# Sixteen dummy matmuls ahead of the first transposes, and a zeroing moved from GpSimd to VectorE

## The chip, the cores and the metric

The kernel runs on one core of one Trainium2 chip. The metric is the device time of one execution in microseconds (us). In the views PE is TensorE (PEld its weight loads), DVE is VectorE, ACT is ScalarE and POOL is GpSimd; L297 is a line of the kernel, x16 a count, `out<-in` what an instruction writes and reads, and `[0.53 <-...]` how long its engine stood idle before it and what ended that.

## The reference, cut to what matters

Attention over landmarks (Nyström) for 8 batches of 8 heads, 576 tokens and 64 dimensions, then a two-layer MLP with a squared ReLU:

```python
q_lm, k_lm = segment means of q and k          # 32 landmarks
A, Bm, C = sm(q, k_lm), sm(q_lm, k_lm), sm(q_lm, k)   # softmaxes
Z = pseudo-inverse of Bm, six Newton steps
x = A @ Z @ C @ v                               # [...] heads joined
h = x @ w_in; r = maximum(h, 0); return (r * r) @ w_out
```

## The kernel before

The program lays out the whole order of each engine by hand. Batch 0 goes through a "head", a list of tokens, before the steady part begins. In the head these tokens matter: `ck` casts k, `tk1` and `tk0` transpose its halves on TensorE, `mk` and `mq` take the segment means of k and q, `cq0` and `cq1` cast q, `w:n` and `w:n:256` issue n dummy matmuls of 512 or 256 columns.

```python
HEAD = ("ck tk1 mk w:1:256 w:1:256 ek1d w:1:256 w:1 tk0 tt w:1 w:1 cq0 cq1 ek0a mq tq0 tq1 lm ...")

def warm(n, width=512):
    z = bds[1].rearrange("p a b c -> p (a b c)")      # a tile zeroed at the start
    for _ in range(n):
        nc.tensor.matmul(idle[:, 0:width], lhsT=z[:, 0:P], rhs=z[:, 0:width], start=True, stop=True)

# token ck
dve(X["k"][:, 0:2], raw[:, 0:2])                      # half of k on VectorE
load_rest(act(X["k"][:, 2:4], raw[:, 2:4]))           # half on ScalarE; later loads wait for it
```

`load_rest` issues, in GpSimd's queue, the weights, v of batch 0, q and k of batch 1 and v of batch 1. Behind the last of these stands the work that the change moves:

```python
with tc.issue_after(behind[0].ins):
    nc.gpsimd.tensor_copy(seg[:, NC4 + 2, :], seg[:, NC4, :])
    for i in range(2):
        ct = const.tile([P, 2, NC4 + 1, P], BF16, name="ct%d" % i)
        nc.gpsimd.memset(ct[:], 0.0)
        cts.append(ct)
```

The two `ct` tiles are used by `ct = cts[b % 2] if b >= DMA_C else None`, and `DMA_C` is 9, so with eight batches nothing reads them. The other line to know is the VectorE copy that brings a later batch's k or q into its natural order (line 283; 282 in the changed kernel):

```python
nc.vector.tensor_copy(X[nm][:], raw)                  # 128 x 2048 bf16, SBUF to SBUF
```

The softmax here doesn't subtract the row's maximum and nothing guards it: scores larger than these inputs give would overflow.

## Time and profile before

| | kernel before |
|---|---|
| runs before the prediction | 265.61, 265.70, 266.66 us |
| profiled run | 266.55 us, of which the span is 264.8 us |
| TensorE (PE) busy | 248.2 us, 94% |
| first transposes start | 8.01 us |
| first landmark scores (line 374) | 14.29 us |
| copy of batch 1's q on VectorE | 2.54 us, from 27.80 us |

The span counts from the first to the last instruction. The lines behind the table, and how to read them, stand in the prediction.

### The profile page before, as it was taken

Reading aid. Unit: us, or ns where it says so; the run is one execution under the profiler, and the core shown is the slowest. Engines: PE = TensorE matmul, PEld = TensorE weight load, DVE = VectorE, ACT = ScalarE, POOL = GpSimd, SP = SyncE. Lnnn points to the kernel's source line nnn. Section 1 sums busy time; section 2 is a strip of 40 time slices with the busy share of each in tenths; the row PEclk is TensorE's granted clock in tenths of the full one; section 3 lists DMA queues with packets and bytes.
Section 4 is the critical chain, followed back from the end, with each engine's and each line's share of the span. In section 5 each row is a group of like instructions: output and inputs, shape, how many; then the busy total and the mean of one; then the engine's idle time right before and its main releaser. Section 6 shows DMA issues by size and latency. Waiting matters only on the chain.

```text
span 264.8 us, 6918 instructions
## 1 busy us (share of the span) xinstructions
PE 248.2 (94%) x2835; PEld 153.7 (58%) x2878; DVE 176.4 (67%) x485; ACT 158.5 (60%) x278; POOL 47.8 (18%) x73
## 2 busy tenths in 40 slices
PE   0799899999999999999999999999999999999994
PEld 0675665467665656566556565666566655555443
DVE  3488986879985779689766589689776884232100
ACT  1364887279666765678457565674777665365210
POOL 7744623302010500700003201320000000000000
PEclk9999999999999999999999999999999999999999
DMA  8999999998159899996829998999911111112122
GB/s 183 161 190 202 209 205 189 214 208 107 32 101 188 98 197 178 184 203 124 121 74 115 172 192 114 128 191 188 159 42 40 42 40 65 56 40 83 40 79 79
DMA packets 69791, 34.65 MB, mean 131 GB/s; under 512 B 37376, under 2 KB 64256, under 8 KB 69760
## 3 DMA queue, kind: packets, MB, share of 16 engines
q0 software_dynamic: 39808, 17.83, 54.2%
q1 hardware_dynamic: 24704, 7.08, 17.3%
q10 hardware_dynamic: 5248, 9.31, 11.3%
q8 instruction: 22, 0.36, 0.6%
q14 instruction: 9, 0.07, 0.1%
HBM read 36.70 MB, written 9.44 MB: 174 GB/s over the span
## 4 chain that ended last, share of the span: by engine, by line
PE 87%; DVE 5%; DMA 2%; issue 2%; ACT 2%; ACTq 0%
PE ops L853 24%; PE h L824 22%; PE n L853 21%; PE n L532 3%; PE g L807 3%; DMA stage<-in_k_dram 2%; PE idle L297 2%; PE n L416 2%; PE n L344 2%; PE n L598 2%; PE n L616 1%; DVE nat L283 1%; DVE gT L829 1%; PE tps L315 1%; PE n L631 1%
## 5 line engine op out<-in xcount | busy, mean ns | idle before, releaser
L828 ACT ACTIVATE r<-h 128x576 bf16<-128x576 f32 x128 | 81.3, 652 | 46.4 <-PE h L824 35.1
L853 PE MATMUL ops<-w_out_bf,gT 128*128 128x512 bf16 (+1 forms) x300 | 76.8, 368 | 0.9 <-issue 0.3
L853 PEld LDWEIGHTS <-gT 128*128 128x128 bf16 x592 | 53.2, 98 | 38.7 <-issue 4.2
L829 DVE TENSOR_TENSOR gT<-r 128x576 bf16<-128x576 bf16 x128 | 54.9, 448 | 26.3 <-ACT r L828 26.1
L824 PE MATMUL h<-AT,G 128*128 128x288 bf16 x448 | 71.0, 286 | 0.2
L853 PE MATMUL n<-w_out_bf,gT 128*128 128x512 bf16 x252 | 69.7, 379 | 1.1 <-issue 0.3
L824 PEld LDWEIGHTS <-G 128*128 128x128 bf16 x512 | 47.7, 97 | 24.3 <-issue 0.8
L705 DVE CAST G<-g 128x1024 bf16<-128x1024 f32 x14 | 17.1, 1224 | 5.4 <-PE g L807 5.4
L864 ACT COPY o_sb<-ops 128x512 f32<-128x512 f32 (+1 forms) x19 | 10.9, 574 | 14.5 <-PE ops L853 14.5
L864 ACT COPY o_sb<-n 128x512 f32<-128x512 f32 x17 | 10.0, 587 | 12.9 <-PE n L853 12.8
L705 ACT CAST G<-g 128x1024 bf16<-128x1024 f32 x14 | 14.2, 1013 | 4.5 <-PE g L807 4.5
L134 POOL DMA_DIRECT2D raw<-in_k_dram x5 | 4.6, 921 | 53.2 <-DVE gT L829 28.1
L532 PEld LDWEIGHTS <-T 128*128 128x128 bf16 x256 | 11.3, 98 | 4.2 <-issue 0.6
L574 DVE TENSOR_REDUCE ra<-EA 128x20 f32<-128x640 f32 (+3 forms) x19 | 13.2, 704 | 0.3 <-ACT EA L562 0.3
L586 DVE TENSOR_TENSOR an<-EA,rra 128x640 bf16<-128x640 f32 (+2 forms) x18 | 13.2, 736 | 0.2
L532 PE MATMUL n<-bd,T 128*128 128x64 bf16 x256 | 12.7, 193 | 0.3 <-issue 0.2
L315 PEld LDWEIGHTS <-nat 128*128 128x128 bf16 x96 | 6.8, 108 | 9.8 <-ACT nat L720 8.0
L537 ACT ACTIVATE EA<-n 128x512 f32<-128x512 f32 x16 | 9.6, 598 | 3.3 <-PE n L532 3.2
L134 POOL DMA_DIRECT2D raw<-in_q_dram x5 | 4.4, 884 | 38.5 <-DVE rc L447 28.1
L537 ACT ACTIVATE EC<-n 128x512 bf16<-128x512 f32 x16 | 9.5, 596 | 3.0 <-PE n L532 1.6
L315 PE MATMUL tps<-ident_bf,nat 128*128 128x128 bf16 x32 | 3.4, 278 | 8.0 <-ACT nat L720 8.0
L824 PE MATMUL h<-AZ,G 128*128 128x288 bf16 x64 | 10.0, 286 | 0.6 <-DVE AZ L797 0.4
(144 smaller groups left out, 294.6 us busy)
## 6 DMA issues: line engine op xcount, KB each, us to landing
out_dram<-o_sb ACTq DMA_DIRECT2D x31, 256.0 KB, 3.1
vm<-in_v_dram POOLq DMA_DIRECT2D x8, 512.0 KB, 10.1
raw<-in_k_dram POOLq DMA_DIRECT2D x5, 512.0 KB, 6.9
raw<-in_q_dram POOLq DMA_DIRECT2D x5, 512.0 KB, 6.1
w_in_bf<-in_moe_w_in_dram POOLq DMA_DIRECT2D x4, 512.0 KB, 12.1
w_out_bf<-in_moe_w_out_dram POOLq DMA_DIRECT2D x4, 512.0 KB, 17.2
out_dram<-o_sb ACTq DMA_DIRECT2D x9, 128.0 KB, 2.4
stage<-in_k_dram SPq DMA_DIRECT2D x1, 1024.0 KB, 6.1
```

What stands on the lines that cost most here:

```text
L134: d = queue.dma_start(dst, src)
L315: nc.tensor.transpose(tps[:, i, p, :], X[nm][:, 2 * half + i, 2 * p:2 * p + 2, :].rearrange("p h d -> p (h d)"), ident_bf[:],)
L532: nc.tensor.matmul(sc[:, c, j, :, :], lhsT=X[nm + "T"][:, c, p, :], rhs=BD[:, 1 if nm == "q" else 0, p, 0:64], start=True, stop=True)
L537: nc.scalar.activation(dst, sc.rearrange("p c j i m -> p c (j i m)"), AF.Exp, scale=SCALE)
L574: nc.vector.reduce_sum(ra[:, quads, lo:hi, :], EA[:, quads, lo:hi, :].rearrange("p q c (h m) -> p q c h m", m=M), axis=AX.X)
L586: on.tensor_tensor(an[:, i, lo:hi, :].rearrange("p c (h m) -> p c h m", m=M), EA[:, i, lo:hi, :].rearrange("p c (h m) -> p c h m", m=M), r ...
L705: (act, dve)[n % 2](G[:, :, n * 512:n * 512 + 512], gg[:])
L824: nc.tensor.matmul(h[:, j, 0:HALF], lhsT=G[:, qd, f * P:(f + 1) * P], rhs=AT[:, qd, a0 + j * HALF:a0 + (j + 1) * HALF], start=(qd == 0), s ...
L828: nc.scalar.activation(r.rearrange("p (j t) -> p j t", j=2), h[:, :, 0:HALF], AF.Relu)
L829: return lambda: nc.vector.tensor_tensor(gT[:, f, o:o + S], r[:], r[:], ALU.mult)
L853: nc.tensor.matmul(ops, lhsT=gT[:, f, t * P:t * P + P], rhs=w_out_bf[:, f, i * n:i * n + n], start=(f == 0), stop=(f == NF - 1))
L864: nc.scalar.copy(o_h, ops)
```

## The change

Two parts. The dummies are to bring TensorE's clock up while k is still loading, so that k's transposes already run at the rate of the later ones (0.056 us each in the kernel before, where the first took 0.107). The zeroing goes to VectorE, which also only waits for k at that time (idle for 3.42 us ahead of its cast of k in the kernel before).

```diff
 HEAD = (
-    "ck tk1 mk w:1:256 ...
+    "w:16 ck tk1 mk w:1:256 ...
@@ constants, ahead of the first cast
     nc.vector.memset(EA[:, :, NC4, :], 1.0)
+    for i in range(2):
+        ct = const.tile([P, 2, NC4 + 1, P], BF16, name="ct%d" % i)
+        nc.vector.memset(ct[:], 0.0)
+        cts.append(ct)
+    nc.vector.tensor_copy(seg[:, NC4 + 2, :], seg[:, NC4, :])
@@ end of load_rest
-        with tc.issue_after(behind[0].ins):
-            nc.gpsimd.tensor_copy(seg[:, NC4 + 2, :], seg[:, NC4, :])
-            for i in range(2):
-                ct = const.tile([P, 2, NC4 + 1, P], BF16, name="ct%d" % i)
-                nc.gpsimd.memset(ct[:], 0.0)
-                cts.append(ct)
```

## The prediction

The early columns give 2.2 us and the copy 1.86, together 4.1; q's load and PE leave 2.9 of these (264.8 to 261.9 us of span), and half of the 0.9 us that lucky runs may have already is taken off, which makes the gain 2.5 and the time 263.2 us. The 5.7 us in it run from PE's first transposes (8.01 us) to the change of their spacing.

> **What bounds the kernel now.** I read the page's busy shares and chain first, then the chain of waits in order of time for the first 40 us, then the timeline of single engines where that chain leaves the TensorE.

> ```profile
> PE 248.2 (94%) x2835; PEld 153.7 (58%) x2878; DVE 176.4 (67%) x485; ACT 158.5 (60%) x278; POOL 47.8 (18%) x73
> ...
> PE 87%; DVE 5%; DMA 2%; issue 2%; ACT 2%; ACTq 0%
> ```

> The TensorE (PE) is busy 94% of the span and carries 87% of the chain that ends last. Past 36 us the chain is nearly all PE, so a microsecond won in the head should still be won at the end. The change touches only the head, so I take that apart. The chain (start, length, piece):

> ```profile
> 0.81 6.08 DMA stage<-in_k_dram
> ...
> 6.91 1.05 ACT nat L720
> ...
> 8.01 1.03 PE tps L315 x8
> 9.04 0.53 PE n L344 x20
> 9.58 1.07 PE idle L297 x4
> 10.64 0.85 PE tps L315 x8
> 11.50 0.43 PE n L325 x4
> 11.92 0.85 PE idle L297 x2
> 12.78 0.53 PE n L344 x20
> 13.31 1.15 PE tps L315 x16
> ...
> 27.89 2.45 DVE nat L283
> 30.34 0.37 DVE gT L829
> ```

> The reader is to see three things. Until 8.0 us the PE waits for k's load and its cast. From 8.0 to 14.3 us the chain is PE without a break, even through the dummy matmuls (line 297), so every PE instruction there counts. At 27.89 us one VectorE (DVE) copy holds the chain for 2.45 us.

> For the first stretch, the groups by shape (mean ns follows the bar) of the dummy with 512 columns, before 13.6 us and then from 14 to 26 us:

> ```profile
> L297 PE MATMUL idle<-bd 128*128 128x512 bf16 x3 | 1.7, 631 | 0.0
> ```
> ```profile
> L297 PE MATMUL idle<-bd 128*128 128x512 bf16 x8 | 2.8, 380 | 0.0
> ```

> The same instruction takes 631 ns early and 380 ns later: the array runs at the slow clock first. The page's clock row prints 9 from the start, so it does not show this. Spacing gives the rate: 8 transposes at 10.44 us span 1.06 us with 0.31 for the last one, so (1.06-0.31)/7 = 0.107 us each; 16 at 30.39 us span 1.07 with 0.23 for the last, so 0.056 each.

> For the DVE copy, the timelines of POOL (GpSimd) and of DVE over 26.5 to 30.6 us:

> ```profile
> 27.36 0.22 POOL L261 COPY seg<-seg 128x32 bf16<-128x32 bf16 x1
> 27.50 2.28 POOL L264 MEMSET ct<- 128x1280 bf16 x2
> ```
> ```profile
> 26.21 0.68 DVE L283 COPY nat<-stage 128x2048 bf16<-128x2048 bf16 x1
> ...
> 27.80 2.54 DVE L283 COPY nat<-stage 128x2048 bf16<-128x2048 bf16 x1
> ```

> The same copy takes 0.68 us at 26.21 and 2.54 at 27.80, where it lies beside the two GpSimd memsets and ends half a microsecond after them (29.78 against 30.34). PE then stands idle 0.66 us for it, and ScalarE 0.90 us behind the DVE work queued after it.

> [...] here PE started at 8.01 and the spacing changes inside the 16 transposes near 13.7, so it took 5.7 us. [...] the trace has 256 uint32 in 0.27 us.

> **The change, part by part.**

> Dummies added: 16 matmuls of 512 columns ahead of the first transposes. They need only the zeroed tile (the two memsets start at 0.99 and together take 1.02 us, so the first ends near 1.5), and PE has nothing to do until 8.0. At the cold 0.427 us each (0.85/2) all 16 take 6.8 us, to 8.4; at the warm rate (0.056 x 4, about 0.22) less. If the clock comes after the same 5.7 us, that is 7.2 us: 13 cold and 3 warm end at about 7.9. They hide in the wait, with a worst case of 0.4 us late. [...]

> What that takes off the chain: the columns that ran cold from 8.0 to 13.7 us. 8 transposes are 1024 columns; the four dummies 3x256+512 = 1280; 8 transposes 1024; 4 tail transposes 512; two dummies 1024; of the last 16 transposes about 5 cold (they span 1.31 us against 1.07 warm, and 0.24/0.051 is 5), 640. Sum 5504. Each 128 columns save 0.107-0.056 = 0.051 us, so 5504/128 x 0.051 = 2.2 us. The means matmuls (32 columns) save nothing: 20 take 0.53 us in the cold and 32 take 0.85 in the warm stretch, the same 0.027 each. What else could hold PE there is early enough: q's casts, now at 10.55 behind other DVE work, can start near 10.1 and end near 10.9, and the q means need them only near 10.7 to 11.0.

> GpSimd work removed: the copy and the two memsets, 2.4 us. Their own time is off the chain (no one waits for them), but the DVE copy loses its 2.54-0.68 = 1.86 us. The gain is cut by a load: POOL's next issue at 26.68 had waited for an earlier load into the stage of q (batch 1), so that q lands at about 26.5. With a head faster by 2.2 the copy would start at 25.6; it must wait until 26.5, and ends at about 27.2 instead of 30.34. So on the DVE both parts together give 3.1 us, not 2.2+1.86 = 4.1. PE gains less: its work before the late transposes ended at 29.72, or 27.5 with the 2.2 off, so they start at about 27.6 instead of 30.39: 2.8. From 30.3 to 36.2 the chain is DVE and ScalarE, so I take between: 2.9 us at 36.2.

> DVE work added: two memsets of 640 uint32, 640/256 x 0.27 = 0.7 us each, 1.4 in all, in its idle 3.49 to 6.91 us; and a 32-column copy of about 0.1 us at 7.6, where DVE is idle again from 8.0 to 9.6. Nothing of it is on the chain.

> Sum for the profiled run: 264.8-2.9 = 261.9 us of span. The profiled execution of before took 266.55 us, but the median is 265.7, so some 0.9 us of what I remove may be lucky already in the quicker executions (an earlier clock, or the copy ahead of the memsets). I take off half of that: a gain of 2.5, 265.7-2.5 = 263.2 us.

> **Rivals.**
> 1. The dummies end too late or the clock still comes late. For: [...] 16 cold ones end at 8.4. Against: even then the transposes follow in the warm. It makes up to 0.4 us, so 263.6.
> 2. Loads become the bound of the head. For: the DMA works at about 200 GB/s from 14 to 58 us, and the loads do not come sooner because PE is quicker; q of batch 1 already cuts 0.9 us. Against: the last w_in piece frees a POOL issue at 31.52 and is needed at 34.92, or 32.0 after; the first w_out piece frees one at 34.06 and is needed at 37.77, or 34.9 after; margins of 0.5 and 0.8 us. If one ends later, 1 us is given back: 264.2.
> 3. The copy's slowness is not the GpSimd memset but, say, its source just landing. For: q had landed only about a microsecond before. Against: the sister copy with the same shape took 0.68. Then only the 2.2 remains, less the quicker half: about 264.
> 4. The gain is eaten later, by ScalarE or DVE becoming the bound. Against: PE's 94% and the later prefetches, which wait for buffers that come free earlier too. It would give 265 to 265.7.

> **Range and chances.** Centre 263.2. Low 262.2 if the whole 2.9 and some 0.6 of stalls go; high 264.6 if rival 2 or 3 holds in part. Faster by over 2% needs 260.4, a gain of 5.3, more than all terms without their overlap (4.1): 0.02. Slower by over 2% has no mechanism: 0.01. Within 2%: 0.97.

> **What will show it.** Dummies of 631 ns from about 1.5 us turning to 380, all done by about 8; the first transposes warm, 0.61 us for eight; the first landmark scores (now 14.29) at about 12.1; the DVE copy of batch 1's q at 0.7 us, starting at about 26.5 and led by a wait for its load; PE's transposes that stood at 30.39 near 27.6. The prediction is wrong if the copy stays over 2 us, if PE shows a new wait for w_in near 32 or w_out near 35, or if the 2.9 us present at 36 us are gone by 60.

## The result, and the profile after

| | before | changed |
|---|---|---|
| runs | 265.61 to 266.66 us, median of 4: 266.00 | 263.55 to 263.73 us, median of 4: 263.71 |
| ratio | | 0.991 (95%: 0.9887 to 0.9933) |
| span of the profiled run | 264.8 us | 262.0 us |

A ratio here is the mean time of one kernel's fast runs over that of the other's in the same rounds, so it is not quite the ratio of the medians. The gain is 0.9%, clear of noise and below the 2% that would count as faster.

The page's busy line and chain of the changed kernel:

```profile
PE 255.2 (97%) x2894; PEld 154.1 (59%) x2894; DVE 176.5 (67%) x488; ACT 158.4 (60%) x278; POOL 45.3 (17%) x70
...
PE 87%; DMA 7%; DVE 2%; POOL 2%; ACT 1%; issue 0%
```

PE's busy time rose by 7 us although the kernel got quicker: the dummies fill 5.8 us that used to be idle. Busy time alone would have told the wrong story. (The instruction count of matmuls also rises by more than 16, because the trace of the kernel before misses some records: 2835 matmuls beside 2878 weight loads, where the changed kernel's has 2894 of each.)

PE's timeline of the changed kernel (start, length, what):

```profile
1.52 5.80 PE L296 MATMUL idle<-bd 128*128 128x512 bf16 x16 [1.52 <-DVE bd L117]
7.85 0.62 PE L314 MATMUL tps<-ident_bf,nat 128*128 128x128 bf16 x8 [0.53 <-ACT nat L719]
8.31 0.55 PE L343 MATMUL n<-seg,nat 128*128 128x32 bf16 x16
...
8.81 0.70 PE L296 MATMUL idle<-bd 128*128 128x256 bf16 x4
9.35 0.61 PE L314 MATMUL tps<-ident_bf,nat 128*128 128x128 bf16 x8
...
11.22 1.05 PE L314 MATMUL tps<-ident_bf,nat 128*128 128x128 bf16 x16
12.11 0.26 PE L373 MATMUL n<-STk,bd 128*128 128x32 bf16 x4
```

The same landmark scores in the kernel before:

```profile
14.29 0.26 PE L374 MATMUL n<-STk,bd 128*128 128x32 bf16 x4
```

The dummies end at 7.32 us, then PE waits 0.53 us for the cast of k. Eight transposes span 0.62 us where they spanned 1.03 to 1.06. The landmark scores come at 12.11 instead of 14.29 us: 2.18 us, of which 0.16 is k's cast starting at 6.75 instead of 6.91 us, a load that landed a little sooner.

VectorE (DVE) of the changed kernel in its first wait and at the two copies of batch 1, and then GpSimd (POOL):

```profile
3.58 1.27 DVE L236 MEMSET ct<- 128x640 uint32 x2
6.75 0.70 DVE L718 CAST nat<-stage 128x1024 bf16<-128x1024 f32 x1 [1.91 <-DMA stage<-in_k_dram]
7.36 0.17 DVE L238 COPY seg<-seg 128x32 bf16<-128x32 bf16 x1
...
24.22 0.70 DVE L282 COPY nat<-stage 128x2048 bf16<-128x2048 bf16 x1
...
26.23 0.69 DVE L282 COPY nat<-stage 128x2048 bf16<-128x2048 bf16 x1 [0.32 <-DMA stage<-in_q_dram]
```
```profile
26.49 0.70 POOL L134 DMA_DIRECT2D vt<-in_v_dram  x1 [1.09 <-DMA stage<-in_q_dram]
29.22 0.68 POOL L134 DMA_DIRECT2D qkt<-in_k_dram  x1 [2.03 <-PE h L823]
```

The zeroing sits in the wait for k. The copy of q takes 0.69 us instead of 2.54, and a new wait of 0.32 us for q's load stands ahead of it. GpSimd, with its memsets gone, only waits longer: its next issue had another wait ahead of it anyway.

The gain can be followed along the whole span. The MLP's ReLU instructions on ScalarE (128 in each trace) start 2.18 us earlier at the first, 3.02 at the seventh (33.30 against 30.28), 3.0 from there to about 160 us, 2.85 from 174 us to the last. The spans differ by 2.8. So of 3.0 us only 0.15 is given back, and the head's microseconds are kept. (The control below gives back 0.4 us between 160 and 174 us, from 3.28 to 2.87; the run with the dummies alone nothing. What takes this was not looked into.) The lead comes in two steps: 2.0 to 2.2 us up to the third ReLU, and 1.0 us more from the fourth on, right after the copy of q.

### The profile page after: what moved, and what is told of

Its sections match the earlier page's. It is cut to its first block, busy times and chain, and to the rows that moved or that the text cites. A ratio compares the mean times of both kernels' runs of the same rounds, so it can differ in the third digit from the quotient of the medians.

```text
span 262.0 us, 6993 instructions
## 1 busy us (share of the span) xinstructions
PE 255.2 (97%) x2894; PEld 154.1 (59%) x2894; DVE 176.5 (67%) x488; ACT 158.4 (60%) x278; POOL 45.3 (17%) x70
## 3 DMA queue, kind: packets, MB, share of 16 engines
q10 hardware_dynamic: 5248, 9.31, 10.9%
## 4 chain that ended last, share of the span: by engine, by line
PE 87%; DMA 7%; DVE 2%; POOL 2%; ACT 1%; issue 0%
PE ops L852 25%; PE h L823 24%; PE n L852 23%; DMA stage<-in_k_dram 7%; PE g L806 3%; PE n L531 3%; PE n L343 2%; PE n L415 2%; PE n L597 2%; PE n L314 1%; PE n L615 1%; PE n L630 1%; PE n L559 1%; POOL w_in_bf L134 1%; DVE G L645 1%; POOL qkt L134 1%
## 5 line engine op out<-in xcount | busy, mean ns | idle before, releaser
L852 PE MATMUL ops<-w_out_bf,gT 128*128 128x512 bf16 (+1 forms) x320 | 81.7, 368 | 0.0
L852 PE MATMUL n<-w_out_bf,gT 128*128 128x512 bf16 x272 | 74.5, 379 | 0.0
L828 DVE TENSOR_TENSOR gT<-r 128x576 bf16<-128x576 bf16 x128 | 54.9, 448 | 26.6 <-ACT r L827 26.5
L863 ACT COPY o_sb<-ops 128x512 f32<-128x512 f32 (+1 forms) x19 | 10.9, 574 | 14.5 <-PE ops L852 14.5
L296 PE MATMUL idle<-bd 128*128 128x512 bf16 (+1 forms) x51 | 13.8, 388 | 1.5 <-DVE bd L117 1.5
L134 POOL DMA_DIRECT2D raw<-in_q_dram x5 | 4.4, 884 | 37.2 <-DVE rc L446 27.2
L415 PEld LDWEIGHTS <-ED 128*128 128x128 bf16 x72 | 6.8, 98 | 6.2 <-DVE EY L454 0.6
## 6 DMA issues: line engine op xcount, KB each, us to landing
w_in_bf<-in_moe_w_in_dram POOLq DMA_DIRECT2D x4, 512.0 KB, 12.1
```

What stands on the lines that cost most here:

```text
L134: d = queue.dma_start(dst, src)
L828: return lambda: nc.vector.tensor_tensor(gT[:, f, o:o + S], r[:], r[:], ALU.mult)
L852: nc.tensor.matmul(ops, lhsT=gT[:, f, t * P:t * P + P], rhs=w_out_bf[:, f, i * n:i * n + n], start=(f == 0), stop=(f == NF - 1))
L863: nc.scalar.copy(o_h, ops)
```

## The experiments

Two theories were at hand for how the parts combine. **A**: what decides is the order in which VectorE's copy and GpSimd's memsets come to the same moment; a quicker head makes the copy come first, and then the place of the zeroing no longer matters. **B**: the two parts are independent terms, the clock (2.2 us) and the slow copy (1.9 us), and simply add up. (The prediction had already cut this sum of 4.1 us to 2.9.) Beside these stood the question whether loads now bound the head.

### The dummies alone

The kernel before with one token added; the zeroing stays where it was.

```diff
-    "ck tk1 mk ...
+    "w:16 ck tk1 mk ...
```

> The kernel before plus the 16 dummies; the zeroing stays on GpSimd. Theory A (loads and issue order): with the head 2.2 us quicker, VectorE reaches the copy of batch 1's q before that q has landed, so it starts just after the landing (about 26.3 us), while GpSimd first issues one more load and starts its memsets about 0.9 us later. The copy gets in first and takes 0.7 us, and the time is that of the full change, 263.7 us within 0.3. Theory B (the sum of two independent terms): the copy is slowed as before to over 2 us, and about 1 us of the gain is missing, 264.7 or more.

Measured: 264.06 us median of 6 (263.26 to 264.63), ratio 0.9938 (0.9902 to 0.9974). VectorE and GpSimd in its profile, taken in the run of 263.26 us:

```profile
26.20 0.70 DVE L283 COPY nat<-stage 128x2048 bf16<-128x2048 bf16 x1 [0.57 <-DMA stage<-in_q_dram]
```
```profile
26.46 0.70 POOL L134 DMA_DIRECT2D vt<-in_v_dram  x1 [1.34 <-DMA stage<-in_q_dram]
27.16 0.22 POOL L261 COPY seg<-seg 128x32 bf16<-128x32 bf16 x1
27.30 2.28 POOL L264 MEMSET ct<- 128x1280 bf16 x2
```

The memsets are there, as long as ever, and the copy takes 0.70 us: it was over 0.26 us before GpSimd's own copy began. Both engines had waited for the same load, and GpSimd had another issue to do first. That is theory A at work in this run: the lead of the ReLUs over the kernel before grows by the same 1.0 us after the copy (2.25 to 3.27), with the memsets still in place. The median is 0.35 us above the full change, a little outside what A allowed and well short of B; whether the slower runs were caught by the memsets was not seen.

### The zeroing alone

The changed kernel without its 16 dummies.

> The full change without the 16 dummies. If the GpSimd memsets were what slowed the copy of batch 1's q, it takes 0.7 us instead of 2.5 and starts at about 27.8 us, and the time lies between the two kernels: 264.4 us (a gain of 1 to 1.8). If the slow copy had another cause (its source just landed), it stays at 2.5 us and the time is that of the kernel before, 266. The spread of its runs should be that of the kernel before (about 1 us)[...].

Measured: 265.13 us median of 6 (264.13 to 265.59), ratio 0.9976 (0.9936 to 1.0016). The copies in its trace (min/median/max ns):

```profile
L282 DVE COPY nat<-stage x2: 682/684/685, 25.7 to 27.2; 128x2048 bf16<-128x2048 bf16 x2
```

Without memsets on GpSimd the copy takes 0.69 us, so its source having just landed was not the cause (the prediction's third rival). The gain is about 0.6 us and its interval touches 1.0, less than the 1 to 1.8 expected. The traces tell what the copy itself costs. The ReLUs on ScalarE just before and just behind it, in the kernel before and then here:

```profile
27.76 1.23 ACT L828 ACTIVATE r<-h 128x576 bf16<-128x576 f32 x2 [0.16 <-PE h L824]
...
30.79 1.19 ACT L828 ACTIVATE r<-h 128x576 bf16<-128x576 f32 x2 [0.90 <-DVE gT L829]
```
```profile
27.20 1.23 ACT L827 ACTIVATE r<-h 128x576 bf16<-128x576 f32 x2 [0.16 <-PE h L823]
...
29.22 1.21 ACT L827 ACTIVATE r<-h 128x576 bf16<-128x576 f32 x2
```

This run is 0.56 us ahead before the copy, as its PE happened to start 0.53 us sooner, and 1.57 us ahead after it. So the slow copy lost VectorE 1.86 us and the MLP 1.0, and that stays to the end (1.46 at the last ReLU). That the timed median shows only 0.6 would fit the kernel before having quick runs without the slow copy (see the two looks at the end); that is not shown.

### The zeroing on GpSimd twice

The kernel before, with each memset issued a second time.

```diff
                 nc.gpsimd.memset(ct[:], 0.0)
+                nc.gpsimd.memset(ct[:], 0.0)
```

> The kernel before with each GpSimd memset issued twice, no dummies. If VectorE's copy is shut out for as long as the memsets run, it takes 2.5 + 2.3 = about 4.9 us and the time rises by 1.5 to 2.3 us to about 268. If the copy's length has another cause it stays at 2.5 us and the time stays at 266.

Measured: 267.39 us median of 4, ratio 1.0065 (1.001 to 1.0121). In the profiled run (268.64 us), VectorE, then GpSimd:

```profile
27.49 4.70 DVE L284 COPY nat<-stage 128x2048 bf16<-128x2048 bf16 x1
```
```profile
27.15 2.28 POOL L264 MEMSET ct<- 128x1280 bf16 x2
29.36 2.28 POOL L265 MEMSET ct<- 128x1280 bf16 x2
```

Four memsets in place of two, and the copy is 2.16 us longer: a dose and its response. The MLP pays all of it: the ReLUs are 0.31 us ahead of the kernel before up to the copy and 1.86 us late after it. The copy ends 0.55 us after the last memset, which is most of the 0.68 us that it takes by itself. The four runs fall in two pairs, 266.07 and 266.13, 268.64 and 268.65. The slow pair, one of which is the profiled run, fits the stall. The quick pair was not profiled; a copy that came ahead of the memsets would explain it.

### No zeroing at all

The changed kernel with the dead tiles left out.

> The full change with the two c-value tiles not zeroed at all (no batch of this kernel uses them, so the result stays right). If the zeroing on VectorE is wholly hidden in its wait for k, the time is 263.7 us within 0.15 and the first cast still starts with the landing of k. If it costs something by holding up GpSimd or the cast, this is 0.3 us or more quicker.

Measured: 263.73 us median of 6, ratio 0.9928 (0.9893 to 0.9962), the time of the full change. VectorE's 1.27 us of memsets are wholly hidden. Since nobody reads the tiles, leaving them out is the cleanest form of this part.

### The change again, as a control

> The full change once more, as the control for the three runs beside it: 263.7 us, and runs within 0.8 us of each other, against over 2 us for the kernel before.

Measured: 263.57 us median of 6 (263.37 to 263.99), ratio 0.9914 (0.9887 to 0.9942). In the same rounds the kernel before ran from 264.31 to 266.82 us. PE's first transposes, then VectorE's copy:

```profile
7.67 0.62 PE L314 MATMUL tps<-ident_bf,nat 128*128 128x128 bf16 x8 [0.45 <-ACT nat L719]
```
```profile
26.32 0.69 DVE L282 COPY nat<-stage 128x2048 bf16<-128x2048 bf16 x1 [0.69 <-DMA stage<-in_q_dram]
```

### Eight dummies

`"w:8 ck ..."` in place of `"w:16 ck ..."`.

> The full change with 8 dummies in place of 16. They end at about 4.95 us, 3.4 us after the start, and PE then idles for 2.9 us. In the traces so far the clock rose 4.4 to 5.8 us after the first matmul. If it needs a span that is busy throughout, 8 are too few: the transposes run at 0.107 us, the clock rises near 13 us, and the time is that of the kernel without dummies, 265.1 us. If a shorter burst is enough, the first transposes are at 0.056 us and the time is 263.7.

Measured: 264.90 us median of 6 (264.77 to 265.33), ratio 0.9965 (0.9937 to 0.9992). PE busy, granted clock and DMA in three stretches (the column after POOL is the clock, those before it are busy us and instructions; the last two, of the DMA, are not used here):

```profile
core 0: us, PE busy (x) PEld busy (x) DVE busy (x) ACT busy (x) POOL busy (x), PEclk, DMA share, GB/s
5.60:8.90 3.30, 1.31 (x32) 1.27 (x33) 1.29 (x5) 1.20 (x2) 1.82 (x7) 1.00 1.65 186
9.00:12.30 3.30, 3.08 (x39) 2.52 (x38) 1.78 (x5) 1.45 (x3) 3.30 (x6) 0.50 0.90 152
12.50:20.00 7.50, 7.38 (x159) 5.53 (x158) 6.55 (x24) 4.05 (x8) 3.50 (x6) 1.00 1.48 191
```

Neither expectation was right. The clock did come up, at 5.54 us in the trace's clock record, 0.43 us after the eight dummies had ended. Then it fell again at 8.95 us, after a stretch in which PE had been busy for only about 40% (1.31 of 3.30 us), and came back at 12.37; both stretches last 3.41 us. The first eight transposes ran fast and the next eight slow (0.62 and 1.06 us). So here it was not enough to raise the clock. Sixteen dummies left a pause of 0.53 us and the clock stayed up (the changed kernel's record has its one rise at 5.97 us); eight left 2.48 and it fell, 1.36 us into the work. Where the limit lies between them, and whether the pause or the low share of busy time decides, was not tested.

### Twenty-four dummies

> The full change with 24 dummies. With the clock up at about 6.4 us they end near 9.1 us, so the first transposes start about 1.2 us late. If the loads of batch 1 bound the head (VectorE waited 0.3 to 0.6 us for q), a part of this delay falls into that wait, and the time rises by about 0.7 us to 264.4. If PE alone bounds the head, it rises by the whole 1.2 us to 264.9.

Measured: 265.49 us median of 6 (263.73 to 265.98). PE in the profiled run (265.60 us):

```profile
1.52 8.23 PE L296 MATMUL idle<-bd 128*128 128x512 bf16 x24 [1.52 <-DVE bd L117]
9.59 0.61 PE L314 MATMUL tps<-ident_bf,nat 128*128 128x128 bf16 x8
```

The clock rose late in this run (7.38 us), so the transposes started at 9.59 us, 1.92 us after those of the control, and not 1.2. Through the head this delay is kept nearly whole: the MLP's first ReLU starts 1.93 us after the control's, the fourth, after the copy, 1.87. So the head hangs on PE, and the wait for q's load takes next to nothing of the delay. At the last ReLU 1.54 us is left, as the control gave back 0.4 us on the way and this run 0.1, and the spans differ by 1.5. The device times differ by 1.92 (265.49 - 263.57, and the profiled runs alike), but that match is chance: four of the six runs here spent 1.9 to 2.6 us outside the span, where every other timed run that lists its span spent 1.7 to 1.8. That is not explained.

### The later loads released earlier

```diff
-                dve(X["k"][:, 0:2], raw[:, 0:2])
-                load_rest(act(X["k"][:, 2:4], raw[:, 2:4]))
+                early = dve(X["k"][:, 0:1], raw[:, 0:1])
+                dve(X["k"][:, 1:2], raw[:, 1:2])
+                act(X["k"][:, 2:4], raw[:, 2:4])
+                load_rest(early)
```

> The full change with VectorE's cast of k cut in two, and the first of the later loads released by the first half (about 7.1 us) rather than by ScalarE's cast (7.8 us). If the loads of batch 1 bound the head, k and q of batch 1 land about 0.6 us earlier, VectorE's wait for q goes from 0.3 to 0.6 us to about nothing, and the time falls by 0.3 to 0.6 us to 263.2. If PE bounds the head the time stays at 263.7; if the earlier load robs batch 0's q of bandwidth, q's casts (at 9.94 us) wait and the time rises.

Measured: 263.50 us median of 6 (263.12 to 263.65), ratio 0.9906 (0.9876 to 0.9936); the control in the same rounds 263.57. VectorE, then PE's late transposes of batch 1:

```profile
25.76 0.69 DVE L282 COPY nat<-stage 128x2048 bf16<-128x2048 bf16 x1
...
28.32 0.46 DVE L830 TENSOR_TENSOR gT<-r 128x576 bf16<-128x576 bf16 x1 [0.76 <-ACT r L829]
```
```profile
27.41 1.06 PE L314 MATMUL n<-ident_bf,nat 128*128 128x128 bf16 x16
```

The same transposes in the control:

```profile
27.28 1.06 PE L314 MATMUL n<-ident_bf,nat 128*128 128x128 bf16 x16
```

The loads landed 0.6 us earlier, VectorE's wait for q is gone, the copy runs 0.56 us earlier, and nothing follows from it: VectorE now waits 0.76 us for ScalarE two instructions on, and PE's transposes stand where they stood. (Their 0.13 us is less than the 0.25 by which PE began later in this run, so at most some 0.1 us was won.) The loads did not bound the head.

That is worth setting beside the chain of the changed kernel, which says otherwise:

```profile
12.38 11.81 DMA stage<-in_k_dram
24.20 0.02 issue
24.22 0.70 DVE nat L282
...
27.72 0.89 PE n L314 x16
```

The chain follows whatever ended last. Here a load landed at 24.20 us, 0.1 to 0.2 us after the other things that its copy needed, so the chain leaves PE for an 11.81 us transfer. In the control, the same kernel, it runs through PE instead. A piece of the chain is a bound only by its margin over the next one, which the chain does not print.

### The zeroing put in the copy's way

The dummies as in the first experiment, with GpSimd's copy and memsets one load earlier in its queue, between the two loads of batch 1's v.

> The 16 dummies with the zeroing on GpSimd, as in e1_dummies_only, but one load earlier in GpSimd's order, so that its memsets run from about 25.2 to 27.5 us and are under way when VectorE comes to the copy of batch 1's q at about 26.2. If it is the order of the two that decides, this copy takes about 1.9 us instead of 0.7 and the time is about 1 us over that of e1 and of the full change, 264.7. If the dummies alone had made the copy immune, it takes 0.7 us and the time is 263.7.

Measured: 265.36 us median of 6 (264.36 to 265.88), ratio 0.9996 (0.9955 to 1.0037). VectorE and GpSimd in the profiled run, its quickest (264.36 us):

```profile
26.32 1.66 DVE L284 COPY nat<-stage 128x2048 bf16<-128x2048 bf16 x1 [0.80 <-DMA stage<-in_q_dram]
```
```profile
25.14 2.28 POOL L203 MEMSET ct<- 128x1280 bf16 x2
```

The dummies do not make the copy immune. Where the memsets are under way when it comes, it takes 1.66 us, and the step of 1.0 us is missing: the ReLUs' lead over the kernel before is 2.38 us ahead of the copy and 2.36 after it. By the medians even more of the gain is lost, nearly all. This is the case that the second part of the change guards against. The slower five runs lose more than the profiled one shows, and what else they met was not seen. (The edit also issues the last load of batch 1 later, at 27.35 us and not 26.46; in the profiled run nothing more is lost after the copy.)

### A try at a better version

VectorE casts the half of k that the first transposes need, 14 dummies, and the first cast of q ahead of an eviction:

```diff
-    "w:16 ck tk1 mk w:1:256 w:1:256 ek1d w:1:256 w:1 tk0 tt w:1 w:1 cq0 cq1 ek0a mq ...
+    "w:14 ck tk1 mk w:1:256 w:1:256 cq0 ek1d w:1:256 w:1 tk0 tt w:1 w:1 cq1 ek0a mq ...
-                dve(X["k"][:, 0:2], raw[:, 0:2])
-                load_rest(act(X["k"][:, 2:4], raw[:, 2:4]))
+                dve(X["k"][:, 2:4], raw[:, 2:4])
+                load_rest(act(X["k"][:, 0:2], raw[:, 0:2]))
```

> A try at a better version: the full change with 14 dummies, VectorE (0.7 us) instead of ScalarE (1.04 us) casting the half of k that the first transposes need, and the first cast of q ahead of the eviction of k's transposes. PE's first transposes start at about 7.4 us instead of 7.7 to 7.9. If PE bounds the head from there, the time falls by 0.3 us to 263.3; if q's second half (landing at about 10 us) holds the q means, no more than 0.1 us is left and the time is 263.5 to 263.7.

Measured: 263.82 us median of 6 (263.56 to 264.39), ratio 0.9945 (0.9902 to 0.9988). PE in its profile:

```profile
7.47 0.63 PE L314 MATMUL tps<-ident_bf,nat 128*128 128x128 bf16 x8
...
10.90 0.36 PE L343 MATMUL n<-seg,nat 128*128 128x32 bf16 x8 [0.42 <-DVE nat L724]
```

The transposes start 0.2 us before the control's, and a wait of 0.42 us for the second cast of q takes that back. A miss: no version was found that is measurably quicker than the change.

### Two more looks at the kernel before

> One more profile of the kernel before, for its spread of over 2 us. If the clock's moment and the order of copy and memsets make it, a slow one (266 or more) shows the clock rising past 13 us and a copy of about 2.5 us, and a quick one (under 265) shows an earlier rise and a copy of 0.7 us that starts ahead of the memsets.

> The same as b1_before_look, as one profile may fall on either side.

Measured: 266.26 and 266.60 us. Both have the slow copy (2.92 and 2.48 us). The clock rose at 12.77 us in the first, not past 13, and at 13.78 in the second. The first has a detail, VectorE and then GpSimd:

```profile
27.13 2.92 DVE L283 COPY nat<-stage 128x2048 bf16<-128x2048 bf16 x1
```
```profile
27.08 0.22 POOL L261 COPY seg<-seg 128x32 bf16<-128x32 bf16 x1
27.22 2.28 POOL L264 MEMSET ct<- 128x1280 bf16 x2
```

The copy begins before the memsets, but 0.05 us after GpSimd's small copy, and it ends 0.55 us after the last of the three, as in the second look (30.19 against 29.64 us). In this trace the 0.09 us by which it came ahead of the memsets did not help it. No quick run of the kernel before was caught in a profile. There are seven of 263.84 to 264.36 us among the 33 that ran beside the timed experiments; those are about as quick as the change. An early clock together with a copy ahead of GpSimd would make such a time, but that is argued and not shown.

## Why the prediction was right

The measured 263.71 us lies in the range, and the gain of 2.5 us that the prediction forecast stands against 2.3 by the medians, 2.8 by the profiled spans and 0.9% by the ratio. Of the half microsecond between 263.2 and 263.71, 0.3 is the base: the median of the kernel before was 265.7 when the prediction was made and 266.0 with the fourth run. The 0.4 us taken off for luckier runs was a guess, and no run tests it; the profiled pair, where nothing is taken off, was forecast at 2.9 of span and gave 2.8.

- **The dummies hide in the wait for k.** Right. They were expected to end at about 7.9 us and ended at 7.32. Their mean is 543 ns, against 631 cold and 379 warm, so (543 - 379)/(631 - 379) x 16 = about 10 were cold, not 13. In other runs the clock came later; with its rise at 7.50 us (the run with earlier loads) they ended at 8.09 and the transposes began without a pause behind them, as the first rival had it, with a cost too small to time.
- **2.2 us less of cold columns.** Right: 2.18 us at the landmark scores, at 12.11 where about 12.1 was expected. Of these 0.16 is the earlier load, so the columns gave 2.0.
- **The copy at 0.7 us, led by a wait for q's load.** Right in both. The cause was shown by doubling it (4.70 us), removing it (0.69 us) and putting it back elsewhere (1.66 us).
- **PE's late transposes at about 27.6.** Right: 27.56. At 36.2 us the gain was to be 2.9 and was 3.0 (the MLP step at 36.21 moved to 33.21).
- **VectorE's memsets cost nothing.** Right: 1.27 us for the two (1.4 expected), hidden; without them the time is the same. They also leave GpSimd alone here: the issue of q's load beside them (2.79 to 4.33 us) takes 1.54 us with them and in the kernel before, which has none there.
- **The weights do not become a wait.** Right: the last w_in piece frees a GpSimd issue at 31.67 us and is needed at 31.93, a margin of 0.3 where 0.5 was expected; the first w_out piece at 34.04 and 34.77. The lead of 3.0 us stands unchanged past 60 us.
- **What failed is an attribution within the sum:** "The gain is cut by a load". The wait for q's load is real (0.32 us, and 0.69 in the control), but with the wait removed the time stayed the same. What cuts the gain is PE, which the prediction also had, in the next sentences, at 2.8. The number came out right because the smaller of two limits was taken.
- **What the sum could not say is how the parts share the gain.** It gave the memsets' removal 1.86 us on VectorE as a term of its own, cut by PE's limit. In the traces the stall is worth 1.0 us, and either part alone removes it: the zeroing by its absence, the dummies because the quicker head brings the copy ahead of GpSimd's work (26.20 against 27.16 us in their run). By the timed runs the zeroing gives 0.6 us alone and at most some 0.3 behind the dummies. The prediction used this order only for the luckier runs ("the copy ahead of the memsets").

One thing it did not mention: the runs of the change (two sets, 263.37 to 263.99 us) spread far less than those of the kernel before (263.84 to 267.23). That fits dummies which take the varying moment of the clock's rise (3.9 to 6.0 us after the first matmul in the traces) into a wait where it costs little.

## What to carry to other kernels

Where TensorE waits for its first load, fill the wait with dummies that end just as the load arrives: with sixteen, ending 0.53 us ahead, the clock stayed up, with eight it fell again 1.4 us into the work, and with 24 the head was 1.9 us late. When two parts of a change both act on one moment, run each alone before adding them: here both remove the same stall of 1.0 us, so the first made the second nearly needless, yet left it as a safeguard. A transfer in the chain of waits bounds the kernel only by its margin over the next thing, and moving that transfer is the test of it.
